# A decode block on one core: the last weight load issued as two loads by partitions

## The chip, the cores and the metric

One NeuronCore of a Trainium2 chip runs the whole kernel. The metric is the device time of one launch in microseconds; lower is better. Times of a kernel are medians over runs.

## The reference, cut to what matters

Two residual blocks follow one another for a batch of 8 single tokens of width 1024: attention over the last 1024 entries of a key and value cache, then a gated feed-forward block of width 3584. All data is fp32.

```python
x = A_x                                            # 8 x 1 x 1024
h = x + attention(layernorm(x), k[:, :, -1024:], v[:, :, -1024:], wq, wo)
g = layernorm(h) @ w_gate                          # 1024 x 3584
u = layernorm(h) @ w_up                            # 1024 x 3584
h2 = h + (gelu(g) * u) @ w_down                    # 3584 x 1024
```

The weights and the caches are about 111 MB, and each byte is used once. The change touches only the very last piece of them, a part of the last 128 rows of `w_down`.

## The kernel before, in words

**Streaming.** Everything that is read from memory goes into one large tile `w`, cut into two buffers `wbuf[0]` and `wbuf[1]`. SyncE's queue (SP) issues all of the weight loads, in program order, and each waits until TensorE is done with the buffer part that it overwrites. First come 12 units of 128 partitions x 64 KB (line 153, `units`), which alternate between the buffers. Then come the pieces of `w_down` that did not fit into the units: two loads of `dn` (line 162) into buffer 0, and into buffer 1 two loads of `tails` (line 169) and two of `ends` (line 179). TensorE works in a loop of passes over the units (`half`, line 219), and VectorE (DVE), ScalarE (ACT) and GpSimd (POOL) prepare its stationary operands.

**The end.** The last contraction, a sum over 3584 rows of `w_down`, is accumulated in PSUM. The output is laid out in NQ = 4 groups of QW = 256 columns, one group per 32 partitions. The last 128 rows of `w_down` (`rows[-1]`) are loaded in two loads cut by columns: `ENDS = (160, 96)` columns of each group. So the first `ends` load is 128 partitions x 640 floats (2,560 B a partition, 320 KB), the second is 128 partitions x 384 floats (1,536 B a partition, 192 KB). Each has its own semaphore, `wl0` and `wl1`, and `move` (line 94) raises the semaphore by 16 when a load has landed.

The end of the program uses them in this order:

- TensorE sums the chunks of `tails` into `acc` (line 436), and ACT copies `acc` to `most` (line 450).
- TensorE waits for `wl0` and multiplies the 160 columns into the tile `fin` (line 461); then it waits for `wl1` and multiplies the 96 columns into the tile `sum` (line 461 again).
- DVE adds `most` and `fin` into 160 columns of `o_fin` (line 464), and then `most` and `sum` into the other 96 columns (line 464 again).
- SP stores the first part of `o_fin` after the first addition, and ACT's queue stores the second part after the second (lines 476 and 477).

The loop of the loads reads

```python
for i, (n, src) in enumerate(zip(ENDS, ends)):
    t = wbuf[1][:, c0:c0 + NQ * n]
    blocks.append((a, n, t, move(f"wl{i}", t, src)))
```

and the loop that uses them

```python
for (c0, n, t, here), d_ps in zip(blocks, (fin, sums[1])):
    for j in range(NQ):
        tok = run("tensor", ... t[:, j * n:(j + 1) * n] ..., here, d1_ok, ...)
    done.append(run("vector", ... most_ok, tok))
```

where `here` is the pair of a semaphore and the value that is waited for.

Of the kernel before, what the change touches and what calls it, by code (L numbers as in the profile page):

```python
# [7 lines left out]
P = 128  # L8
# [22 lines left out]
ENDPARTS = (2, 1)  # L31
ENDS = (160, 96)
AHEAD = 3
PAD = 128


# [8 lines left out]
class Flow:  # L45
# [37 lines left out]
    def run(self, engine, make, *waits, mark=True, gives=None):  # L83
        ins = self.start(engine, make, waits)
        if gives is not None:
            ins.then_inc(*gives)
            return None
        if not mark:
            return None
        self.done[engine] += 1  # L90
        ins.then_inc(self.own[engine], 1)
        return self.own[engine], self.done[engine]

    def move(self, name, out, src, *waits, engine="sync", sem=None):
        s = self.sem(name) if sem is None else sem
        self.start(engine, lambda e: e.dma_start(out, src), waits).then_inc(s, 16)  # L96
        return s, 16


def decode_block(nc, x, units, dn, tails, ends, outs):  # L100

    fl = Flow(nc)
    run, move = fl.run, fl.move
# [3 lines left out]
    def sb(name, *shape):  # L107
        return nc.alloc_sbuf_tensor(name, list(shape), F32).ap()
# [37 lines left out]
    def half_b(k, h=1):  # L146
        return at_mark["b", k, h]
# [5 lines left out]
    for u in range(UNITS):  # L153
        k, i = divmod(u, 2)
# [14 lines left out]
    for i, n in enumerate(ENDPARTS):  # L169
        here = move(f"we{i}", wbuf[1][:, c0:c0 + n * D], tails[i], half_b(nb - 1))  # L170
# [6 lines left out]
    blocks = []  # L177
    a = 0
    for i, (n, src) in enumerate(zip(ENDS, ends)):
        t = wbuf[1][:, c0:c0 + NQ * n]  # L180
        blocks.append((a, n, t, move(f"wl{i}", t, src)))
        c0 += NQ * n
        a += n

# [203 lines left out]
    for k, n in enumerate(SETS):  # L388
# [16 lines left out]
        t = turned[:, 0:N].rearrange("p (i m) -> p i m", m=P)  # L405
# [19 lines left out]
    for ch in range(2):  # L425
        p0 = 32 * (2 + ch)
# [25 lines left out]

    ahead = sb("ahead", 1, AHEAD)
    for i in range(AHEAD):
        run("vector", lambda e: e.memset(ahead[:, i:i + 1], 0.0), arrived[last - 1][1], d1_ok)
# [111 lines left out]
```

## Time and profile before

| | |
|---|---|
| median of 3 runs | 263.92 us (263.63 to 263.96) |
| the profiled execution, its own time | 263.59 us |
| its span, first to last instruction | 262.3 us |
| data read from memory | 111.18 MB, 424 GB/s over the span |
| share of 16 DMA engines' time, SP's queue | 98.4% |
| TensorE busy | 141.3 us, 54% of the span |
| DVE busy | 43.8 us, 17% |

The span starts with the first instruction and ends with the last. The time of the execution is 1.29 us longer than its span. TensorE, DVE and ACT are idle for much of the span, and the DMA engines are not: the kernel moves its data at the rate at which it comes, and what the other engines do after the last data has landed is added to that.

In the views "PEld" is TensorE's loading of the stationary operand, "SPq" and "ACTq" are the queues of SyncE and ScalarE, which issue transfers, and "<-" after a time of idleness names what ended it. A matmul of fp32 shows as two instructions.

### The profile page before, as it was taken

To read this page: it belongs to the slowest core of one execution; us is meant where nothing else is said; L and a number is where in the kernel's file an instruction comes from. 1 tells how busy PE (TensorE), PEld (TensorE's weight loads), DVE (VectorE), ACT (ScalarE), POOL (GpSimd) and SP (SyncE) were. 2 spreads that over 40 slices of the span, in tenths; PEclk is the share of its full clock that TensorE was granted. 3 is DMA by queue.
4 is the path that set the end of the run, shared out by engine and by line. 5 is a ranking of instruction groups with operands and counts; after the bars stand their busy time and mean duration, and the time that the engine had idled before them with its cause. 6 is when DMAs were issued, how large, how long until landed. Compare 5 with 4: busy or idle time off the path is not lost. (4 is left out here: it accounts for less than half of the span.)

```text
span 262.3 us, 2262 instructions
## 1 busy us (share of the span) xinstructions
PE 141.3 (54%) x972; PEld 45.1 (17%) x972; DVE 43.8 (17%) x115; ACT 13.5 (5%) x19; POOL 7.7 (3%) x18
## 2 busy tenths in 40 slices
PE   0025805926606927707908508827709809409986
PEld 0021201212101312102302102122102202103232
DVE  0340200240100140400410100264100300100522
ACT  1000000000120010000000200000300000200000
POOL 5000100100000000100100000000000000000000
PEclk9999985986965995956966965975956956858999
DMA  8997997999799799979979998997999999799895
GB/s 320 485 470 330 480 480 340 460 480 460 340 480 480 320 480 480 460 340 480 480 320 480 480 420 380 480 480 320 480 480 400 400 480 480 320 440 480 370 424 226
DMA packets 2896, 111.31 MB, mean 424 GB/s; under 512 B 456, under 2 KB 712, under 8 KB 976
## 3 DMA queue, kind: packets, MB, share of 16 engines
q1 hardware_dynamic: 2736, 111.23, 98.4%
q10 hardware_dynamic: 160, 0.08, 0.1%
HBM read 111.18 MB, written 0.13 MB: 424 GB/s over the span
## 5 line engine op out<-in xcount | busy, mean ns | idle before, releaser
L227 PE MATMUL sum<-w,still 128*32 128x512 f32 x832 | 116.3, 721 | 96.8 <-PEq L214 96.8
L227 PEld LDWEIGHTS sum<-w,still 128*32 128x32 f32 x832 | 32.5, 130 | 176.8 <-issue 176.7
L245 PE MATMUL turned<-ident,source 128*128 128x128 f32 x64 | 10.4, 315 | 20.9 <-PEq L214 20.9
L245 PEld LDWEIGHTS turned<-ident,source 128*128 128x128 f32 x64 | 8.3, 161 | 26.2 <-issue 26.2
L240 PE MATMUL turned<-y_sb,add 128*32 128x512 f32 x24 | 11.3, 592 | 0.9 <-PEq L214 0.9
L326 DVE TENSOR_REDUCE nmax<-sum 128x1 f32<-128x1024 f32 x2 | 2.4, 1224 | 28.4 <-PE sum L227 28.4
L401 DVE TENSOR_TENSOR up<-up,sum 128x512 f32<-128x512 f32 (+1 forms) x2 | 1.4, 684 | 32.2 <-PE sum L227 32.2
L297 DVE TENSOR_SCALAR q<-sum 128x512 f32<-128x512 f32 x2 | 1.4, 692 | 25.7 <-PE sum L227 25.7
L282 DVE COPY still<-turned 128x1024 f32<-128x1024 f32 x4 | 4.7, 1219 | 4.2 <-PE turned L245 4.2
L391 DVE TENSOR_TENSOR gate<-gate,sum 128x512 f32<-128x512 f32 (+1 forms) x2 | 1.4, 686 | 23.8 <-PE sum L227 23.8
L353 DVE SCALAR_TENSOR_TENSOR o<-sum,share,o 128x128 f32<-128x128 f32 x12 | 4.2, 350 | 4.2 <-PE sum L227 3.8
L350 DVE TENSOR_SCALAR o<-sum,share 128x128 f32<-128x128 f32 x2 | 0.7, 350 | 22.9 <-PE sum L227 22.9
L328 ACT ACT_TABLE_LOAD x1 | 1.3, 1283 | 59.0 <-DVE nmax L326 59.0
L357 POOL MEMSET still<- 128x1024 f32 x2 | 1.9, 952 | 74.3 <-PE sum L227 74.3
L240 PEld LDWEIGHTS turned<-y_sb,add 128*32 128x32 f32 x24 | 2.6, 110 | 8.7 <-issue 8.7
L369 DVE TENSOR_TENSOR y_sb<-y_sb,sum 128x512 f32<-128x512 f32 x1 | 0.7, 689 | 16.0 <-PE sum L227 16.0
L370 DVE TENSOR_TENSOR y_sb<-y_sb,sum 128x512 f32<-128x512 f32 x1 | 0.7, 689 | 15.8 <-PE sum L227 15.8
L302 POOL MEMSET still<- 128x1024 f32 x2 | 1.9, 958 | 46.4 <-PE sum L227 46.4
L328 ACT ACTIVATE source<-sum,nmax 128x1024 f32<-128x1024 f32 x2 | 2.2, 1114 | 18.8 <-PE turned L245 18.8
L368 ACT COPY y_sb<-sum 128x512 f32<-128x512 f32 x1 | 0.6, 586 | 50.7 <-PE sum L227 50.7
L313 DVE COPY still<-turned 128x16 f32<-128x16 f32 x32 | 2.7, 161 | 2.1 <-PE turned L245 2.1
L390 ACT COPY gate<-sum 128x512 f32<-128x512 f32 (+1 forms) x2 | 1.2, 584 | 30.6 <-PE sum L227 30.6
(64 smaller groups left out, 43.3 us busy)
## 6 DMA issues: line engine op xcount, KB each, us to landing
w<-dn SPq DMA_DIRECT2D x1, 6144.0 KB, 24.1
w<-dn SPq DMA_DIRECT2D x1, 2048.0 KB, 28.7
w<-tails SPq DMA_DIRECT2D x1, 1024.0 KB, 13.3
w<-tails SPq DMA_DIRECT2D x1, 512.0 KB, 14.2
w<-ends SPq DMA_DIRECT2D x1, 320.0 KB, 14.6
w<-units SPq DMA_DIRECT2D x12, 29.5
w<-ends SPq DMA_DIRECT2D x1, 192.0 KB, 14.5
out<-o_fin SPq DMA_DIRECT2D x1, 80.0 KB, 1.6
```

Source lines behind the costliest of these rows:

```text
L227: ins = PE.matmul(sums[i][32 * j:32 * j + 32, h * N:(h + 1) * N], still[i][:, 32 * s:32 * s + 32], wbuf[i][:, s * N:(s + 1) * N], start=(c ...
L240: ins = PE.matmul(turned[0:32, ch * N:(ch + 1) * N], add2[:, ch, :], y_sb, start=True, stop=True)
L245: ins = PE.transpose(turned[:, n * P:(n + 1) * P], source[:, n * P:(n + 1) * P], ident)
L282: run("vector", lambda e: e.tensor_copy(still[i].rearrange("p (c j m) -> p c j m", c=NC, j=NQ), turned.rearrange("p (c m) -> p c m", c=NC) ...
L297: tok = run("vector", lambda e: e.tensor_scalar(q_sb, sums[hf][:, 0:N], scale, None, op0=ALU.mult), done(0, 0))
L302: cleared.append(run("gpsimd", lambda e: e.memset(still[hf], 0.0), done(0)))
L313: run("vector", lambda e: e.tensor_copy(to[:, :, b, s, a, REP * b:REP * b + REP].rearrange("p k (h i) -> p k h i", h=2), frm[:, s, a * HB ...
L326: tok = run("vector", lambda e: e.tensor_reduce(out=nmax, in_=sums[hf], axis=AX.X, op=ALU.max, negate=True), done(1))
L328: p_ok = run("scalar", lambda e: e.activation(source, sums[hf], AF.Exp, bias=nmax, accum_out=tot), tok, at_mark["t", 1 + hf])
L353: tok = run("vector", lambda e: e.scalar_tensor_tensor(out, o3[:, b], share[hf][:, b:b + 1], o_sb, op0=ALU.mult, op1=ALU.add), tok, done(2 ...
L357: cleared[hf] = run("gpsimd", lambda e: e.memset(still[hf], 0.0), done(2))
L391: tok = run("vector", lambda e: e.tensor_add(gate[:rows], gate[:rows], sums[0][:rows, N:2 * N]), tok, half_a(4 + k))
```

## The change

The second `ends` load, 128 partitions x 384 floats, becomes two loads: first partitions 120 to 127 (8 partitions, 12 KB), then partitions 0 to 119 (120 partitions, 180 KB). Both raise the same semaphore `wl1`, and the value that is waited for is the sum, 32, where it was 16. The first `ends` load stays one load of 128 partitions. Nothing else is changed.

```diff
 AHEAD = 3
+SHARES = (((0, P),), ((120, P), (0, 120)))
 PAD = 128
...
     for i, (n, src) in enumerate(zip(ENDS, ends)):
         t = wbuf[1][:, c0:c0 + NQ * n]
-        blocks.append((a, n, t, move(f"wl{i}", t, src)))
+        here = None, 0
+        for p0, p1 in SHARES[i]:
+            s, val = move(f"wl{i}", t[p0:p1], src[p0:p1], sem=here[0])
+            here = s, here[1] + val
+        blocks.append((a, n, t, here))
         c0 += NQ * n
         a += n
```

SP's queue at the end of the program, before (sizes are partitions x floats):

```order
L96 DMA w<-dn 128x12288 [waits tensor_done]
L96 DMA w<-dn 128x4096
L96 DMA w<-tails 128x2048 [waits tensor_done]
L96 DMA w<-tails 128x1024
L96 DMA w<-ends 128x640
L96 DMA w<-ends 128x384
L96 DMA out<-o_fin 128x160 [waits vector_done]
```

The same place with the change (all lines below the new constant have other numbers):

```order
L97 DMA w<-dn 128x12288 [waits tensor_done]
L97 DMA w<-dn 128x4096
L97 DMA w<-tails 128x2048 [waits tensor_done]
L97 DMA w<-tails 128x1024
L97 DMA w<-ends 128x640
L97 DMA w<-ends 8x384
L97 DMA w<-ends 120x384
L97 DMA out<-o_fin 128x160 [waits vector_done]
```

One issue is added, between the first `ends` load and the rest of the second; the other engines have the same instructions in the same order.

## Rows read from the trace of the kernel before

**Rows 1.** The page: engines, DMA in 40 slices, chain by engine.
```profile
span 262.3 us, 2262 instructions
...
PE 141.3 (54%) x972; PEld 45.1 (17%) x972; DVE 43.8 (17%) x115; ACT 13.5 (5%) x19; POOL 7.7 (3%) x18
...
DMA  8997997999799799979979998997999999799895
```

**Rows 2.** Chain of waits, from 244.88 on: start us, us, what.
```profile
244.88 14.56 DMA w<-ends
259.44 0.04 issue
259.49 0.48 PE fin L461 x8
259.96 0.40 PE sum L461 x8
260.37 0.02 issue
260.39 0.26 DVE o_fin L464
```

**Rows 3.** Timeline, 244 to 262 us: start us, us, instruction, idle before and its releaser.
```profile
244.03 0.80 SPq L96 DMA_DIRECT2D w<-tails  x2
...
244.88 0.92 SPq L96 DMA_DIRECT2D w<-ends  x2
...
258.67 0.26 PEld L436 LDWEIGHTS acc<-w,at 128*32 128x32 f32 x8 [0.17 <-DMA w<-tails]
...
259.46 0.37 ACT L450 COPY most<-acc 128x256 f32<-128x256 f32 x1 [18.28 <-PE acc L436]
259.48 0.16 PEld L461 LDWEIGHTS fin<-w,at 128*32 128x32 f32 x8 [0.56 <-DMA w<-ends]
259.49 0.48 PE L461 MATMUL fin<-w,at 128*32 128x160 f32 x8
259.95 0.16 PEld L461 LDWEIGHTS sum<-w,at 128*32 128x32 f32 x8 [0.31 <-DMA w<-ends]
259.95 0.37 PE L461 MATMUL sum<-w,at 128*32 128x96 f32 x8
260.03 0.32 DVE L464 TENSOR_TENSOR o_fin<-most,fin 128x160 f32<-128x160 f32 x1 [1.17 <-PE fin L461]
260.38 0.35 SPq L96 DMA_DIRECT2D out<-o_fin  x1
260.39 0.26 DVE L464 TENSOR_TENSOR o_fin<-most,sum 128x96 f32<-128x96 f32 x1
260.68 0.35 ACTq L96 DMA_DIRECT2D out<-o_fin  x1
```

**Rows 4.** Busy time by stretch at the end; last two columns: DMA share, GB/s.
```profile
258.90:259.00 0.10, 0.10 (x9) 0.03 (x3) 0.00 (x0) 0.00 (x0) 0.00 (x0) 1.00 1.00 365
259.00:259.10 0.10, 0.10 (x8) 0.00 (x0) 0.00 (x0) 0.00 (x0) 0.00 (x0) 1.00 0.81 292
259.10:259.20 0.10, 0.10 (x8) 0.00 (x0) 0.00 (x0) 0.00 (x0) 0.00 (x0) 1.00 0.55 185
259.20:259.30 0.10, 0.10 (x4) 0.00 (x0) 0.00 (x0) 0.00 (x0) 0.00 (x0) 1.00 0.25 77
259.30:259.35 0.05, 0.05 (x4) 0.00 (x0) 0.00 (x0) 0.00 (x0) 0.00 (x0) 1.00 0.09 31
259.35:259.40 0.05, 0.05 (x4) 0.00 (x0) 0.00 (x0) 0.00 (x0) 0.00 (x0) 1.00 0.09 31
259.40:259.45 0.05, 0.01 (x2) 0.00 (x0) 0.00 (x0) 0.00 (x0) 0.00 (x0) 1.00 0.01 0
```

**Rows 5.** The timeline near 248 us, DVE: two operations back to back.
```profile
247.78 1.23 DVE L423 TENSOR_TENSOR down<-down,sum 32x1024 f32<-32x1024 f32 x1
249.04 0.88 DVE L427 COPY rest<-down 32x512 f32<-32x512 f32 x2
```

**Rows 6.** What SP's queue waited for: us in total, times, longest.
```profile
SPq L96 <- DVE o_fin L464: 14.9, 1, 14.9
```

**Rows 7.** The page, DMA issues: KB, us from issue to landing.
```profile
w<-ends SPq DMA_DIRECT2D x1, 192.0 KB, 14.5
out<-o_fin SPq DMA_DIRECT2D x1, 80.0 KB, 1.6
out<-o_fin ACTq DMA_DIRECT2D x1, 48.0 KB, 1.6
```

**Rows 8.** Timeline, start of the program: the one load of 8 partitions.
```profile
1.70 1.21 ACTq L96 DMA_DIRECT2D x_sb<-x  x1
...
10.33 1.27 DVE L260 BATCH_NORM_STATS2 ln_bn<-x_sb 32x6 f32<-32x512 f32 x2 [7.83 <-DMA x_sb<-x]
```

## The prediction

> **What bounds the kernel now.** I read the page first. The DMA engines are busy in nearly every slice of the span, while TensorE is busy for 54% of it and DVE for 17% [rows 1]. So the kernel is bound by its loads, and the change adds no byte to them. What it can move is the very end: the time between the landing of the last bytes and the last store.
>
> The chain of waits comes next [rows 2]. It ends in a landing of an `ends` load at 259.44, TensorE's `fin` product, its `sum` product, and DVE's second addition, which ends at 260.65. After it come ACT's store, issued at 260.68 [rows 3] and landing 1.6 us after its issue [rows 7], which is 262.3, the end of the span. The store and the addition before it do not change. The question is when the second addition can start.
>
> The timeline shows who waits for what [rows 3]. The `fin` product starts at 259.49, when the first `ends` load has landed. The `sum` product starts at 259.95; its weight loads were held for 0.31 us by the second `ends` load. That second load is the one that is cut in two. But DVE has work of its own in that time: its first addition starts at 260.03 and takes 0.32, so DVE is not free before 260.35. The second addition starts at 260.39. **The second load's landing therefore has only 0.04 us to give**, however early it comes.
>
> The table by stretches shows how that load ends [rows 4]. Until 259.00 all 16 DMA engines are busy (share 1.00). Then the share falls to 0.81, 0.55 and 0.25 in steps of 0.1 us, and from 259.30 to 259.40 it is 0.09 with 31 GB/s. In 0.05 us that is 31 x 0.05 = 1.55 KB, one partition's row of this load (1,536 B). One engine of 16 is a share of 0.06. So at the end a single engine is still moving rows when the others are done, for some 0.10 us. The last landing is that engine's.
>
> **The change part by part.**
>
> *The added issue on SP.* Two `ends` issues take 0.92 us together, 0.46 each [rows 3]; the one load of 8 partitions in this program took 1.21 us to issue, on ACT's queue at the start [rows 8]. So the added issue costs SP 0.46 to 1.21 us. I take 0.46, the same queue at the same place. It is hidden: after the last `ends` issue SP waits 14.9 us for DVE's first addition [rows 6], and the loads ahead in the queue keep the DMA engines busy until 259. The 192 KB landed 14.5 us after their issue [rows 7]; being handed over up to 1.21 us later does not make them later. If that cover were gone, the cost would be those 0.46 to 1.21 us. Nobody is queued behind the issue but the store of 260.38.
>
> *The rows themselves.* The same 192 KB moves. Between the releases of the `fin` and the `sum` product lie 259.95 - 259.48 = 0.47 us, the time of this load behind the one before it. With 128 partitions on 16 engines that is 8 rows an engine, so **0.47 / 8 = 0.059 us for a row** on one engine.
>
> *A fixed cost for one more transfer.* Loads that are queued back to back show none: the releases by the last `tails`, the first `ends` and the second `ends` lie at 258.67, 259.48 and 259.95 [rows 3], 0.81 us apart for 320 KB and 0.47 for 192 KB, or 405 and 418 GB/s, as fast as the 424 GB/s of the whole span. A cost per transfer would make the smaller one slower by the byte, and it isn't. I take nothing. The other end is a transfer that is not overlapped at all: the store's 1.6 us from issue to landing [rows 7].
>
> [...]
>
> *Which engine gets which rows.* No row shows it, so I bound the landing from both sides. At best the lone engine loses its rows and the load lands when the others end, at about 259.30 and not 259.40, so 0.10 us earlier. At the next worse, the lone engine is given one row more: 0.06 us later. Cases in which the rows crowd on few engines are a rival below. I take the best case, because the 8 rows that go first are just one engine's share of 128, and the other 120 are 15 engines' shares.
>
> [...]
>
> *The sum.* The landing comes 0.10 us earlier, so the `sum` product starts at 259.85 and ends, in place of 260.37 [rows 2], at 260.27. TensorE is free for it: the `fin` instructions overlap it, as they do now. What is late next is DVE, busy with the first addition until 260.35. Two DVE operations back to back leave 0.03 us between them (247.78 + 1.23 = 249.01, the next at 249.04 [rows 5]), so the second addition starts at 260.38, not 260.39. **The sum is 0.01 us**, with bounds of nothing and of 0.04. The first addition waits for `fin`, that for the first `ends` load, and that one is ahead in the same queue and unchanged.
>
> Against the profiled execution (263.59 us, span 262.3) this gives 263.58. That execution is 0.33 us under the median of 263.92, and the runs shown scatter over 0.33 us, so I predict from the median: 263.92 - 0.01, **263.9 us**. A measurement of this kernel can tell about 0.2% from no change, which is 0.53 us.
>
> **The rivals.**
>
> 1. *The lone engine gets more.* If it is among those that carry one of the 8 rows, its landing comes at 259.97, the `sum` product and everything behind it 0.06 us later: 263.98 us. For it: eight engines of sixteen may share these rows. Against it: nothing in the rows. Also if the lone engine keeps just its eight rows, the time stays at 263.92. Neither can be told from the forecast by the time; the wait of 0.31 us ahead of `sum` tells them apart.
>
> 2. *Half speed: fewer engines, or slower rows.* The `sum` product has no slack to the later side, so any lateness of the landing counts. If the 120 rows went by 8 engines, with the 8 rows on the same ones, an engine would have 15 + 1 rows: 16 x 0.059 = 0.94 us in place of 0.47, so 264.39 us. Rows that take twice as long, because 15 engines write other sets of partitions than 16 did, give the same. To pass 0.53 us an engine needs (0.47 + 0.53) / 0.059 = 17 rows, so the 120 rows must be on 7 engines or fewer. On one engine they would take 120 x 0.059 = 7.1 us, which is 270.5. Against it: every load of 128 partitions here keeps all engines busy, and 120 is no stranger a size. For it: this program has no load of 120 partitions.
>
> 3. *The two loads do not overlap: slower.* If the load of 0 to 119 started only when that of 120 to 127 had landed, as if each were alone, `wl1` would reach 32 later by an unhidden transfer, 1.6 us [rows 7]: 263.92 + 1.6 = 265.5 us. It decides as soon as the gap between the two is over 0.53 us. For it: the two raise one semaphore and are issued back to back. Against it: the four loads before them are issued back to back too, and follow each other at full rate [rows 3].
>
> 4. *The change frees more than I see: faster.* It needs an earlier `fin`, which depends on the first `ends` load alone. Nothing in the change reaches that, and the second load can give 0.04 us at most. A time under 263.4 would be a mechanism that no view shows.
>
> **How the numbers follow.** The forecast has 0.62. Rival 1, with its variant of no relief, has 0.21. Rival 2 has 0.09: 0.07 at about 264.4, of which I count half as told from no change since it lies at the bound, and 0.02 at more. Rival 3 has 0.05. Rival 4 has 0.03. So faster by over 0.2% has 0.03, slower by over 0.2% has 0.05 + 0.02 + 0.03 = 0.10, and within it 0.87. The range starts at 263.5, the forecast less the scatter of the runs shown and a little, and ends at 264.4, which takes in rivals 1 and 2; the rest beyond it is about 0.1.
>
> **What would show it.** In the profile of the changed kernel SP has three `ends` issues of about 0.46 us each, and still waits over 14 us after them. In the stretches near 259.3, relative to the release of `fin`, the tail of one lone engine is gone. The weight loads ahead of `sum` wait about 0.2 us where they waited 0.31, and `sum` starts about 0.37 us after `fin` where it was 0.47. The second addition follows the first by 0.35 us where it was 0.36, released by DVE's own end and no longer by TensorE. The prediction is wrong if `sum` starts later after `fin` than 0.53 us (rivals 1 to 3 by how much), or if `fin` itself moves, or if the time is outside the range while these gaps are as said.

## The result and the profile after

The changed kernel takes **264.03 us** (median of 22 runs, 263.72 to 264.90) where the kernel before takes 263.68 us (22 runs, 263.53 to 264.17): a ratio of 1.0015, 95% interval 1.0009 to 1.0022. It is 0.35 us slower. That is within 0.2%, but clear of no change, and on the other side of a forecast of 0.01 us sooner. The profiled execution of the changed kernel took 264.0 us, with a span of 262.7; the one of before took 263.59 with a span of 262.3. Ratios here and below are of fast runs alone; of the later kernels, the one cut at partition 64 and the one cut at partition 8 had one slow run each of eleven (343.5 and 293.6 us), which moves their medians by less than 0.04 us.

The timeline of the changed kernel at the end, in the columns of [rows 3]:

```profile
245.27 1.24 SPq L97 DMA_DIRECT2D w<-ends  x3
...
258.70 0.27 PEld L441 LDWEIGHTS acc<-w,at 128*32 128x32 f32 x8 [0.16 <-DMA w<-tails]
...
259.73 0.16 PEld L466 LDWEIGHTS fin<-w,at 128*32 128x32 f32 x8 [0.76 <-DMA w<-ends]
...
260.28 0.32 DVE L469 TENSOR_TENSOR o_fin<-most,fin 128x160 f32<-128x160 f32 x1 [1.38 <-PE fin L466]
260.38 0.16 PEld L466 LDWEIGHTS sum<-w,at 128*32 128x32 f32 x8 [0.49 <-DMA w<-ends]
...
260.82 0.25 DVE L469 TENSOR_TENSOR o_fin<-most,sum 128x96 f32<-128x96 f32 x1 [0.22 <-PE sum L466]
261.11 0.35 ACTq L97 DMA_DIRECT2D out<-o_fin  x1
```

Up to the release by the last `tails` load the two executions run alike (258.70 against 258.67 in [rows 3]). Then two waits are longer, and each gets a letter here. **Gap A**, from the last `tails` release to the start of the `fin` weights, is 259.73 - 258.70 = 1.03 us; before it was 0.81. **Gap B**, from there to the `sum` weights, is 0.65; before it was 0.47. Together they are 1.68 against 1.28, so `sum` comes 0.40 us later after the `tails`. The second addition is 0.43 later (260.82 against 260.39), and ACT's store 0.43 (261.11 against 260.68). The rest of the kernel's end is as before. Gap A is the surprise: it ends with the landing of the *first* `ends` load, which the change doesn't touch.

The packets of that first load are not slower. A DMA packet here is one partition's row of a load, and the trace has the start and the time of each. The 128 packets of 2,560 B take 104 ns on average (105 before), and the last of them ends 0.82 us after the last packet of `tails`, as before. What is later is the landing, the last increment of the load's semaphore. It came 0.50 us after the last packet before, and comes 0.70 us after it now. The last load has both: its last packet ends 0.06 us later, counted from the `tails`, and its landing comes 0.78 us after that packet where it was 0.46.

The table by stretches of the changed kernel, as [rows 4]:

```profile
258.90:259.00 0.10, 0.10 (x8) 0.07 (x4) 0.00 (x0) 0.00 (x0) 0.00 (x0) 1.00 0.92 335
259.00:259.10 0.10, 0.10 (x11) 0.00 (x0) 0.00 (x0) 0.00 (x0) 0.00 (x0) 1.00 1.15 338
259.10:259.20 0.10, 0.10 (x8) 0.00 (x0) 0.00 (x0) 0.00 (x0) 0.00 (x0) 1.00 1.01 184
259.20:259.30 0.10, 0.10 (x7) 0.00 (x0) 0.00 (x0) 0.00 (x0) 0.00 (x0) 1.00 0.90 184
259.30:259.40 0.10, 0.10 (x4) 0.00 (x0) 0.00 (x0) 0.00 (x0) 0.00 (x0) 1.00 0.39 78
259.40:259.50 0.10, 0.06 (x4) 0.00 (x0) 0.00 (x0) 0.00 (x0) 0.00 (x0) 1.00 0.19 46
```

Read the last two columns together; a packet counts whole in the stretch in which it starts. Before, a share of 1.00 went with 365 GB/s. Here a share of 1.01 goes with 184 GB/s, and 0.90 with 184. So the packets that start there take twice as long for their bytes. The packet records say it of single rows: before, the 128 packets of 1,536 B took 67 ns on average and none over 79; with the change they take 82 ns on average, 31 of them take over 100, and the longest 148.

The chain of waits of the changed kernel now runs through `sum` alone, and `fin` has left it (compare [rows 2]):

```profile
246.16 14.17 DMA w<-ends
260.33 0.04 issue
260.38 0.42 PE sum L466 x8
260.80 0.02 issue
260.82 0.25 DVE o_fin L469
```

### The profile page after: what moved, and what is told of

Its sections match the earlier page's. It is cut to its first block, busy times and chain, and to the rows that moved or that the text cites. A ratio compares the mean times of both kernels' runs of the same rounds, so it can differ in the third digit from the quotient of the medians.

```text
span 262.7 us, 2263 instructions
## 1 busy us (share of the span) xinstructions
PE 145.3 (55%) x972; PEld 46.0 (17%) x972; DVE 43.8 (17%) x115; ACT 13.5 (5%) x19; POOL 7.7 (3%) x18
## 5 line engine op out<-in xcount | busy, mean ns | idle before, releaser
L232 PE MATMUL sum<-w,still 128*32 128x512 f32 x832 | 120.2, 743 | 92.9 <-PEq L219 92.9
L232 PEld LDWEIGHTS sum<-w,still 128*32 128x32 f32 x832 | 33.4, 133 | 176.0 <-issue 175.9
L245 PE MATMUL turned<-y_sb,add 128*32 128x512 f32 x24 | 11.3, 592 | 0.9 <-PEq L219 0.9
```

The source lines that it names most:

```text
L232: ins = PE.matmul(sums[i][32 * j:32 * j + 32, h * N:(h + 1) * N], still[i][:, 32 * s:32 * s + 32], wbuf[i][:, s * N:(s + 1) * N], start=(c ...
L245: ins = PE.matmul(turned[0:32, ch * N:(ch + 1) * N], add2[:, ch, :], y_sb, start=True, stop=True)
```

## The experiments

Two theories stood against each other after this. **Places:** in a load of other than 128 partitions, engines write partitions at the same time that share a place of SBUF (the on-chip memory that holds `w`), and get in each other's way. **Count:** nothing of that kind, but only one transfer more (its own cost) or one row more on eight engines. Both are guesses: no record here shows which engine writes which partition, or which are written together.

**The cut made large.** Six of the twelve units (those of buffer 1, 8.4 MB each) are cut as whole loads, by three different cuts. TensorE's gate for them counts both loads.

```diff
-        move(f"u{u}", wbuf[i], units[u][:, 0:BUF], free, sem=go[i])
+        for p0, p1, a, b in (CUTS if i else ((0, P, 0, BUF),)):
+            move(f"u{u}", wbuf[i][p0:p1, a:b], units[u][p0:p1, a:b], free, sem=go[i])
...
-                half(1, [(0, (go[1], 17))])
+                half(1, [(0, (go[1], 33))])
```

`CUTS` stands here for the three cuts, one in each kernel: partitions 120 to 127 and 0 to 119; partitions 0 to 63 and 64 to 127; and two halves of the columns. Expected:

> The cut of the change, made large: each of the six units of buffer 1 (8.4 MB, one lands every 19.35 us) is loaded as partitions 120 to 127 and partitions 0 to 119. Theory P (rows of a load that is not of 128 partitions are written slower, because its engines write places of SBUF that collide): the units take up to twice their time, up to 6 x 19.35 = 116 us more, at least well above 15 us; and packets of this kernel take longer than 0.31 us per 8 KB-sized row part of before. Theory R (only the count of rows: eight engines have nine rows of 2.4 us instead of eight): 6 x 2.4 = 14.5 us more. Theory T (a transfer more costs a fixed 0.2 to 0.4 us): 6 x 0.4 = at most 2.4 us more.

> The six units of buffer 1 are loaded as partitions 0 to 63 and 64 to 127. All engines have equal rows. Theory P: each half is written slower, up to 116 us more in all. Theory R: no change. Theory T: at most 2.4 us more.

> The six units of buffer 1 are loaded as two loads of all 128 partitions, the first and the second half of the columns. Theory P: no change, since the partitions are those of before. Theory R: no change. Theory T: six transfers more, at most 2.4 us more.

Measured: **488.39, 393.17 and 264.18 us**, against 263.68; each of the three is one run. The cut by columns, with as many transfers, costs 0.5 us for six units. The cut by partitions costs 224.7 and 129.5 us, more than the 116 I had set as an upper end. The stretches of the kernel with 64 and 64 partitions, busy times first, DMA share and GB/s last:

```profile
44.00:62.00 18.00, 0.00 (x0) 0.00 (x0) 0.00 (x0) 0.00 (x0) 0.00 (x0) 0.50 0.92 197
64.00:80.00 16.00, 11.83 (x76) 3.71 (x76) 4.07 (x34) 0.00 (x0) 0.96 (x1) 0.82 1.04 451
```

From 44 to 62 us it loads a half of 64 partitions, at 197 GB/s; from 64 to 80 a whole unit of buffer 0 passes at 451. The kernel with 8 and 120 partitions:

```profile
36.00:68.00 32.00, 0.00 (x0) 0.00 (x0) 0.00 (x0) 0.00 (x0) 0.00 (x0) 0.50 0.95 197
```

The 120 rows go at 197 GB/s with the engines busy by 0.95. A packet of 64 KB takes 2.42 us in the kernel before (the median of 1,536; 3.41 at most); from 36 to 66 us here all of them take 4.98 to 5.13 us. The slowest of the run are six groups of fifteen, the first fifteen packets of each cut unit, with 8.7 to 11.3 us. Eight of each fifteen are the eight neighbouring rows at most, so the rows of the 120 that start beside them are held up too. So rows of 64 and of 120 partitions take twice as long, and eight neighbouring rows, with what runs beside them, about four times. Count is out: nine rows for eight would have been 14.5 us, and as many transfers cut by columns cost 0.5. Why loads of 64 and of 120 partitions both go at 197 GB/s, no run shows.

**One transfer more, at the end.** The last load is cut by columns and not by partitions:

```diff
-SHARES = (((0, P),), ((120, P), (0, 120)))
+SHARES = (((0, 640),), ((0, 192), (192, 384)))
...
-            s, val = move(f"wl{i}", t[p0:p1], src[p0:p1], sem=here[0])
+            s, val = move(f"wl{i}", t[:, p0:p1], src[:, p0:p1], sem=here[0])
```

> The last load is cut in two by columns (192 and 192 of 384 floats), both of 128 partitions, both on the one semaphore: one transfer more, as in the change, but no other partitions. Theory P: as before, within 0.1 us of 263.7; fin starts 0.81 us after the release of the last tails product and sum 0.47 us after fin. Theory T: as the change, 264.0, with gaps of 1.03 and 0.65 us. Theory R: as before.

Measured: 263.76 us, ratio 1.0004 (0.9995 to 1.0013), gaps 0.84 and 0.49. The transfer itself, with its issue and its completion, costs 0.05 us in the gaps and nothing that the time can tell.

**Which rows do the harm.** Four runs take the two loads apart. Two leave the last load whole and add a load of eight rows into a spare tile ahead of it; one issues the eight rows ahead of the `tails`; one swaps the two loads. The expectations set two guesses against each other: P8 puts the harm to `fin` down to the eight rows, which would crowd where the late engine (the lone one of the prediction) still writes; P120 puts all of the harm down to the 120 rows. The diff shows the table of parts alone; where rows go to a spare tile or are issued early, `move` gets the other target or place. The comments are added here.

```diff
-SHARES = (((0, P),), ((120, P), (0, 120)))
+SHARES = (((0, P),), ((120, P), (0, P)))      # eight rows go to a spare tile
+SHARES = (((0, P, 1),), ((96, P, 4), (0, P, 1)))   # the same, every fourth partition
+SHARES = (((0, P),), ((0, 120),))             # 120 to 127 issued ahead of the tails
+SHARES = (((0, P),), ((0, 120), (120, P)))    # swapped
```

> The last load stays whole, and ahead of it goes a load of the same 8 rows (partitions 120 to 127) into a spare tile at the same partitions, on the same semaphore. The output does not use the spare tile. [...] Theory P120 (the 120 rows on 15 engines do all of the harm): fin after 0.81 to 0.87 us as before, sum after 0.47 to 0.53. Time 263.9 by P8, 263.75 by P120.

> As the run before it, but the eight rows are partitions 96, 100, and so on to 124. Theory P8, if what counts is which partitions are written together: the rows no longer crowd, fin after 0.81 to 0.87 us, sum after 0.47 to 0.53, time 263.75. If eight rows on eight engines are slow wherever they go, as in the run before: fin after about 1.0 us, 263.9.

> The two loads of the change, but the eight rows are issued ahead of the tails loads, and only the 120 rows come last. Theory P8: fin after 0.81 to 0.87 us, and sum later than 0.47 after it by what the 120 rows alone cost, at most the 0.65 of the change; time 263.7 to 263.9. Theory P120: fin after about 1.0 us and sum after 0.65, 264.0.

> The two loads of the change in the other order, 0 to 119 first and 120 to 127 last. [...] Theory P120: fin after 1.03 us, sum after 0.65, 264.0.

Then the 120 rows alone, two other cuts by partitions, and the change itself once more, each with its own `SHARES` (`(0, 120)` alone; `(0, 64), (64, P)`; `(0, 8), (8, P)`; as in the change):

> Only the load of partitions 0 to 119 is issued; partitions 120 to 127 of the last load are left out, so that part of the output is not the reference's. 12 KB less are moved. If the 120 rows on 15 engines do harm by themselves: fin starts 0.85 to 0.95 us after the release of the last tails product (0.81 before) and sum about 0.60 us after fin (0.47 before), time about 263.95. If it takes both loads to do harm: gaps of 0.81 and 0.47 us or less, time 263.7 or less.

> The last load is cut into partitions 0 to 63 and 64 to 127; each engine has 8 rows, as before. Theory of places (rows that are written together crowd, as in the large test, where this cut halved the rate): sum comes 0.6 to 0.95 us after fin, fin 0.85 to 1.05 after the tails, time 264.1 to 264.3. If only the count of rows and transfers matters: gaps of 0.84 and 0.49 us as with the cut by columns, time 263.75.

> The two loads of the change with other partitions: 0 to 7 first, then 8 to 127. If the harm to fin is that the eight rows crowd in the places of the late engine: fin after 0.88 to 0.95 us instead of 1.03, sum after 0.60 to 0.65, time 263.95. If the place doesn't matter: gaps of 1.03 and 0.65 and 264.05.

> The change itself once more, for the scatter of its gaps between two executions: fin 0.95 to 1.10 us after the tails, sum 0.60 to 0.70 us after fin. The swapped order had 1.23 and 0.61, which no theory here gives; if this execution differs from the first by 0.2 us, that is scatter.

The results, with the kernels above among them (us; ratio to before with its 95% interval):

| the last load | A | B | A + B | time | ratio |
|---|---|---|---|---|---|
| whole (before) | 0.81 | 0.47 | 1.28 | 263.68 | |
| cut by columns | 0.84 | 0.49 | 1.33 | 263.76 | 1.0004 (0.9995 to 1.0013) |
| whole, and 8 spread rows | 0.88 | 0.44 | 1.32 | 263.79 | 1.0005 (0.9996 to 1.0014) |
| whole, and 8 neighbouring rows | 1.01 | 0.44 | 1.45 | 263.84 | 1.0007 (0.9998 to 1.0016) |
| 8 rows early, 120 last | 0.90 | 0.60 | 1.50 | 264.11 | 1.0015 (1.0006 to 1.0024) |
| 120 alone | 0.98 | 0.61 | 1.59 | 263.97 | 1.0010 (1.0001 to 1.0020) |
| 64 and 64 | 1.21 | 0.40 | 1.61 | 264.12 | 1.0019 (1.0010 to 1.0029) |
| 8 and 120 (the change) | 1.03 | 0.65 | 1.68 | 264.03 | 1.0015 (1.0009 to 1.0022) |
| the change, once more | 1.27 | 0.30 | 1.57 | 264.00 | one run |
| 120 and 8 (swapped) | 1.23 | 0.61 | 1.84 | 264.14 | 1.0016 (1.0007 to 1.0025) |
| 0 to 7, then 8 to 127 | 1.24 | 0.45 | 1.69 | 264.07 | 1.0013 (1.0004 to 1.0022) |

The gaps come from rows like these two, of the kernel with 8 neighbouring rows and a whole load, and of the one with 8 spread rows:

```profile
258.66 0.26 PEld L442 LDWEIGHTS acc<-w,at 128*32 128x32 f32 x8 [0.17 <-DMA w<-tails]
259.67 0.16 PEld L467 LDWEIGHTS fin<-w,at 128*32 128x32 f32 x8 [0.75 <-DMA w<-ends]
260.11 0.16 PEld L467 LDWEIGHTS sum<-w,at 128*32 128x32 f32 x8 [0.28 <-DMA w<-ends]
```

```profile
258.69 0.26 PEld L442 LDWEIGHTS acc<-w,at 128*32 128x32 f32 x8 [0.17 <-DMA w<-tails]
259.57 0.16 PEld L467 LDWEIGHTS fin<-w,at 128*32 128x32 f32 x8 [0.62 <-DMA w<-ends]
260.01 0.16 PEld L467 LDWEIGHTS sum<-w,at 128*32 128x32 f32 x8 [0.28 <-DMA w<-ends]
```

What follows:

- Every kernel in which the last piece is cut by partitions, or the 120 rows go alone, has A + B of 1.50 to 1.84 and takes 263.97 to 264.14 us. Each whose last load covers all 128 partitions has 1.28 to 1.45 and takes at most 263.84. The 120 rows alone, with 12 KB less to move, are 0.3 us later than the whole load, so they suffice for most of the harm.
- The harm doesn't need fewer than 16 landings a load. With 64 and 64 partitions the semaphore has 32 increments by landings, 16 for each load, as a load of 128 partitions has, and A + B is 1.61 all the same.
- Eight neighbouring rows ahead of a whole load add 0.17 us to A + B, eight spread rows 0.04. In the times the two can't be told apart (263.84 and 263.79), so their share rests on one profile each, and 0.13 us between them is little more than the scatter below.
- My split of the harm, the eight rows to gap A and the 120 rows to gap B, fell. The swapped order and the cut at 8 have 1.23 and 1.24 in gap A, where I expected at most 0.95. And the change itself, once more, has 1.27 and 0.30 where it had 1.03 and 0.65:

```profile
258.67 0.27 PEld L441 LDWEIGHTS acc<-w,at 128*32 128x32 f32 x8 [0.16 <-DMA w<-tails]
259.94 0.16 PEld L466 LDWEIGHTS fin<-w,at 128*32 128x32 f32 x8 [1.01 <-DMA w<-ends]
260.24 0.16 PEld L466 LDWEIGHTS sum<-w,at 128*32 128x32 f32 x8
```

How the lateness divides over the two landings changes from execution to execution; in these two its sum differs by 0.11 us (1.68 and 1.57). What decides it in one execution was not found.

The packet records of all eleven profiles part the rows from the landings, as above. The last packet of the first `ends` load ends 0.81 to 0.83 us after the last packet of `tails` in each of them, so that load's packets are never late. Its landing comes after its last packet by:

| kernel | landing after the last packet, us |
|---|---|
| before, cut by columns, 8 spread rows | 0.50 to 0.53 |
| 8 neighbouring rows, 8 early, 120 alone, the change | 0.65 to 0.70 |
| 64 and 64, swapped, cut at 8, the change once more | 0.86 to 0.91 |

What gap A grows by is this time, to within 0.06 us. At the last load both parts vary: in the change 0.06 us were added in the packets and 0.32 in the landing after them, in its second execution 0.26 in the packets and nothing after them. So a load can land later although its own packets don't end later. That its increment is held up by slow writes of the next load's rows would fit; no view shows what happens between a packet's end and the increment.

**The side on which they crowd.** In all of these, neighbouring partitions were also neighbouring rows in memory. Four kernels exchange the sides: ahead of each of the six units of buffer 1 goes a load of eight rows of 24 KB into a spare tile, read from one set of rows and written to one set of partitions.

```diff
+        if i == 1:
+            move(f"s{u}", spare[TO], units[u][FROM, 0:3 * BUF // 8], free, sem=go[i])
         move(f"u{u}", wbuf[i], units[u][:, 0:BUF], free, sem=go[i])
```

> Ahead of each of the six whole units of buffer 1 goes a load of eight rows of 24 KB into a spare tile. They are read from the rows of partitions 96, 100, to 124 and written to partitions 120 to 127. At full speed a row takes 24/64 of the 2.42 us that a 64 KB packet takes, 0.91 us, and 6 x 0.91 = 5.4 us are added. If the crowding is on the written side, the eight rows take four times as long, 3.6 us, and up to 6 x 3.6 = 22 us are added, at least 12. If it is on the read side: about 5.4 us.

> As the run before it with the sides exchanged: read from the rows of partitions 120 to 127, written to partitions 96, 100, to 124. If the crowding is on the written side: about 5.4 us are added. If it is on the read side (rows that lie side by side in memory): 12 to 22 us.

> The added eight rows are both read from the rows of partitions 96, 100, to 124 and written to these partitions. The run that wrote spread and read neighbouring rows added 14.2 us, more than the 5.4 expected of full speed. If those 14.2 us are the price of any added row beside a whole unit, and the read side counts for nothing: 14 us again. If reading neighbouring rows was a part of it: clearly less, 5 to 10 us.

> The added eight rows are both read from the rows of partitions 120 to 127 and written to these partitions. The run that wrote crowded and read spread added 26.8 us. If only the written side counts: 27 us again. If the read side counts too: clearly more, 30 to 40 us.

Time added to the run of before beside each, and the mean time of a 24 KB packet (0.91 us at the rate of the 64 KB packets):

| written to | read from spread rows | read from neighbouring rows |
|---|---|---|
| spread partitions (96, 100, to 124) | 11.3 us, 1.49 us | 14.2 us, 1.46 us |
| neighbouring partitions (120 to 127) | 26.8 us, 3.03 us | 26.5 us, 3.04 us |

Each kernel is a single run. The written side decides: it makes 12 to 16 us, and with it given the packets take the same time whichever rows they are read from. The read side makes 2.9 us at most. That a spread load still adds 11.3 us, with packets at 1.49 us, where full speed would be 5.4 and 0.91, I had not foreseen. Its rows too are written beside those of a whole unit, which may be why; that was not tried. The sides were exchanged for eight rows alone, so for loads of 64 and 120 partitions the written side is argued from these and not shown.

## Why the prediction was wrong

*What bounds the end.* Right for lateness. `sum`'s landing has no room to the later side, and a lateness goes through to the store: 0.40 us in A + B became 0.43 at the store and 0.41 in the profiled executions' times (264.0 against 263.59). Wrong for a gain. The 0.04 us that the landing had to give, and so the sum of 0.01, took from [rows 5] that DVE's second addition follows the end of the first by 0.03 us. But of the two operations in [rows 5] the second reads `down`, which the first writes. The two additions of the end write different columns and don't read each other's, and in the second execution of the change one starts 0.24 us after the other, before that one's 0.32 are over:

```profile
260.49 0.32 DVE L469 TENSOR_TENSOR o_fin<-most,fin 128x160 f32<-128x160 f32 x1 [1.63 <-PE fin L466]
260.73 0.24 DVE L469 TENSOR_TENSOR o_fin<-most,sum 128x96 f32<-128x96 f32 x1
```

So by these rows a landing 0.10 us earlier could have been worth up to that, an estimate. It didn't come earlier.

*The added issue on SP.* Right. Three issues take 1.24 us together, 0.41 each, and SP waits 14.1 us for DVE after them (14.9 in [rows 6]):

```profile
SPq L97 <- DVE o_fin L469: 14.1, 1, 14.1
```

*No fixed cost for one more transfer.* Right: the cut by columns, with as many transfers as the change, shows 0.05 us in the gaps where the change shows 0.40.

*Which engine gets which rows.* No run shows it. The records of the semaphore `wl1` show counts of landings: before, it has 16 increments by landings; with the change it has one at each of the two issues (246.25 and 246.67) and then 23, which is 8 and 15.

```
last increments of wl1, us   before: 259.779 259.790 259.905   change: 260.231 260.301 260.335
```

The 15 fits the 15 engines that the prediction took for the 120 rows; that an increment is one engine's, no record shows. The lone last landing, 0.115 us behind the one before it, is gone with the change (0.034). That fits a late engine that has no rows in the last load any more, but the rows' longer times spread the landings too, so it isn't shown.

*The time of a row, and of its landing.* **This is the step that failed.** I took 0.059 us for a row whichever load it belongs to, and the bounds for the landing as one engine's rows less or one row more. In the changed load a packet took 82 ns on average where it was 67, and up to 148. I also read the end of the last row as the landing and left out the time between them, though [rows 4] has the last row start by 259.40 and [rows 3] the release at 259.95. That time was 0.46 us before, and with the change it grew to 0.78. So the landing of `sum` came 0.40 us later after the `tails`, and not 0.10 earlier or 0.06 later.

Rival 2 named slower rows ("because 15 engines write other sets of partitions than 16 did") as its second variant, and I gave it 0.09 in all. I put it low on the ground that 120 is no stranger a size than 128, which no row supported. That its 0.47 us lies near the 0.40 measured is luck: it has rows twice as slow and all of the lateness between `fin` and `sum`, where gap B grew by 0.18 us and in the second execution shrank. The one other load of 8 partitions in the program, which I had used for its issue only, writes every fourth partition, and its packets go at full speed (4 KB in 159 ns; those of the last `tails`, 162); it could not have warned of neighbouring ones.

*`fin` is ahead in the same queue and unchanged.* Wrong as well. Gap A grew by 0.22 us in one execution and by 0.46 in the other, though the packets of that load ended as before; its landing came later behind them. The two loads do overlap: rows of the last load start at 258.50, and the last row of the first ends at 258.99. So the loss was not at `sum` alone. Both signs that the prediction had named for being wrong came: `sum` starts later after `fin` than 0.53 us, and `fin` itself moves.

*Rivals 1 and 3.* Rival 1 (one row more, 0.06 us) is in the size of the spread rows (0.04 in A + B), not in that of the change. Rival 3 (1.6 us, no overlap) didn't happen.

## What to carry to other kernels

Cut a load by columns and keep all partitions: a further transfer cost 0.05 us at the end of a queue, a cut by partitions 0.3 to 0.5 us for 192 KB and up to 37 us for 8.4 MB. When a load is reshaped, compare the GB/s at full DMA share before and after; a busy share alone hides that the engines move half (197 GB/s at a share of 0.95, where a whole unit passes at 451 and 1.04). A transfer's neighbours in the queue are part of its price: the load *before* it can land later though its own packets are not slower (0.70 us after its last packet where it was 0.50). And the end of the last packet is not the landing: here 0.46 to 0.50 us lay between them even before the change.

## What the runs showed that was not expected

- In every load by SP of the kernel before, the last of the 16 increments lags 0.115 to 0.152 us behind the one before it, from the first unit (22.42 and 22.56 us) to the last `ends` load. It doesn't grow with the bytes, so it is no lower rate. In other executions the lag is another (0.17 to 0.23 us with the units cut by columns). Where it comes from, and whether it is always the same engine's, was not found.
- A load to eight neighbouring partitions slowed whole loads beside it: with eight such rows of 24 KB ahead of each unit of buffer 1, single 64 KB packets of the units took up to 6.1 us, where their median before is 2.42 and their longest 3.41.
